# Attention and gated MLP on one core: side tiles for remade columns, earlier loads for the last rows, another split of the last row

## The chip, the core and the metric

The kernel runs on one core of a Trainium2 chip. The time is the device time of one execution in microseconds (us), and the median of the runs counts. Engines: TensorE (PE, with its weight loads PEld), VectorE (DVE), ScalarE (ACT), GpSimd (POOL), and SyncE (SP), which issues most of the transfers. Each engine works through its own list of instructions in a fixed order; an instruction that waits holds up those behind it on its engine.

## What is computed

The input x has 2048 rows of 512. Two branches read its layer norm; the result joins them.

```python
xn = _layernorm(x, axis=-1)
s = _A_ref(xn, A_wqkv, A_wo)      # attention: 32 heads of 16, each row looks at 8 rows
                                  # (itself and 2, 4, ... 14 rows back), softmax, then @ wo
g = _silu(_B_ref(xn, ...))        # below
return x + s * g

# _B_ref: F = 1792, Fh = 896
z = _gelu(x @ w_in)
z1 = z[..., :Fh]
z2 = _layernorm(z[..., Fh:], axis=-1)
g = einsum("ts,bsf->btf", w_sp, z2) + b_sp[None, :, None]   # 2048 x 2048 times 2048 x 896
return (z1 * g) @ w_out
```

Everything is float32.

## The kernel before

**Products.** Each product splits its operands into a high and a low part of type F32R and adds three matmuls (high x high, high x low, low x high). The splitting is done by ACT (the high part, a copy, line 195) and DVE (the low part, a subtraction, line 197) after a raw block has come in (line 169). Raw blocks lie in a ring of four buffers, `raws`; the parts of one block in *side tiles*, `wts`, with a tag for high (`wh`) and one for low (`wl`). Eight *wide* buffers (`t4`) of 128x1024 hold whatever is large: the rows of z2 (`zt_j`), sums, biases, gates (`sg_i`) and x rows (`x3_i`) by turns.

**Stages, in the order PE meets them.** The projection to q, k and v (L385 to L387), whose results leave through `stage` tiles to DRAM. For some columns the layer norm is remade: `xs_k` is high plus low, times a row statistic `rb`, split again (L497 to L502). The rows of z2 (L699 to L727): PE fills PSUM banks in turn, eight of them, ACT empties each with the gelu (L728), DVE takes statistics (L737, L738) and finishes them for two row tiles at once (`mvz`, L740), POOL turns the variance into a factor and an offset (`nmz`, L741 to L743), ACT normalises (L749), and DVE combines row tiles (L762) that SP stores to `t_d` (L768, L769). The large product with w_sp runs as sums of block products (`g`, L820) whose bank starts from a bias seed that ACT writes (L838), with block sums `sa`, `sb`, `sr` made on DVE (L393) and stored to `sums_d`. The product with w_out gives b (L1062 to L1075), stored to `b_d`. At the end comes the product of the attention rows with wo (`s`, the same lines L1062 to L1064 of the projection helper).

**The last stage (L1078 to L1125).** Rows are taken in pairs of 128-row tiles, i = 0, 2, ... 14, in four groups of two pairs. A group's attention rows `ol` are loaded (L802) and split into `o_0h`, `o_0l` to `o_3h`, `o_3l`. For each pair the gate `sg_i` and the x rows come in (`fetch_pair`, L1084 and L1085), the gate goes through silu on ACT (L1107), DVE multiplies the product by the gate (L1117) and adds x (L1122, or L1119 for the last pair), and the result is stored (L1123, L1120). A pair's two loads are *paced*: they wait for a given group's o_3h on ACT. The very last row is done in two pieces, so that the first can be finished while PE makes the second.

**Attention.** It runs on DVE and POOL beside all this, in 32 units of low priority (`attention()`). A unit loads keys and queries (L552, L553), multiplies (`pr`, L573) and sums (`lg`, L580), masks the logits of the first rows by memsets (L595), makes the softmax, weighs the values (`pv`, L617) and adds them up, and stores to `o_d` (L642). Most of its tiles have one buffer.

**Order.** The program is written in source order with priorities, and a scheduler that simulates the engines sets each engine's list. So an edit can move instructions far from its own lines.

Of the kernel before, what the change touches and what calls it, by code (L numbers as in the profile page):

```python
# [57 lines left out]
def kernel(  # L58
# [419 lines left out]
    for j in range(11, NT):  # L478
        if j + 2 < NT:
            fetch_cols(j + 2)  # L480
        if j == NT - 3:
            rb = raws.tile([P, 512], F32, tag="raw", name="rb", bufs=RAW)
            rbv = rb.rearrange("p (j q) -> p j q", j=JC)
            pin(nc.sync.dma_start(rbv, mv_d[:JC, 1].unsqueeze(0).to_broadcast([P, JC, P])))
        turned = column_tile(j)
        if j == 12:
            for i in range(HT - 2):
                pool_sums(1, i, early_tile, turned, SYNC)
        low_x(j - 1, cols[j - 1])
        if j % 2:  # L490
            pair(0, j - 5)
# [38 lines left out]
    def attention():  # L530
# [15 lines left out]

        def load_qk(u):
            sub, h = units[u]
            ks[u] = ap_.tile([P, HWIN, CS], F32, tag="k", name=f"k_{sub}_{h}")
            qs[u] = ap_.tile([P, NH, CS], F32, tag="q", name=f"q_{sub}_{h}")  # L550
# [37 lines left out]
        def shifted(u):  # L588
            sub, h = units[u]
            n = NH * HS  # L590
            lg = lgs[u]
            for w in range(1, W):
                if DIL * w > h * NH:
                    front = min(DIL * w - h * NH, NH) * HS
                    line(nc.vector.memset(lg[0:1, W - 1 - w, :front], MASKED))  # L595
# [179 lines left out]
    for i in range(HT + 2):  # L775
        if i in (1, 3):
            raw_sums(1, HT - 2 + i // 2)
        if i < HT:
            raw_z[i] = [t4(f"zt_{j}").rearrange("p i t -> p (i t)")[:, :FH] for j in (i, HT + i)]
            for h in range(2):  # L780
                for j, zt in zip((i, HT + i), raw_z[i]):
                    z2_half(j, h, zt)
                if i == HT - 1 and h == 0:
                    spatial[0, 1] = spatial_block(0, 1)
        if i == 5:
            b_a = t4("b_a")
# [292 lines left out]
        return t.rearrange("(p j) d -> p j d", j=NT)[:, j : j + 2, :]  # L1079

    def fetch_pair(i, after=None):
        gt, xt = t4(f"sg_{i}"), t4(f"x3_{i}")
        for ins in (
            nc.sync.dma_start(gt, b_d[rows_of[i] // 2]),  # L1084
            nc.sync.dma_start(xt, rows_at(x, rows_of[i])),  # L1085
        ):
            if after:
                tc.add_manual_dep(ins.ins, after.ins.name, SYNC, reason="paced")
        return gt, xt
# [9 lines left out]
    for i in range(0, NT, 2):  # L1099
# [5 lines left out]
        gt, xt = fetched[i]  # L1105
        gt, xt = fetched[i]
        nc.scalar.activation(gt, gt, AF.Silu)  # L1107
        for a in range(2):
            jj = (j0 + a) % NJ
            last = i + a == NT - 1  # L1110
            for p_ in range(1 + last):
                cols_ = slice(p_ * D // 2, (p_ + 1) * D // 2) if last else slice(0, D)
                psu = proj(
                    KB, lambda k: [t[:, jj * P : (jj + 1) * P] for t in os_[k]], wos, f"s_{j0 + a}_{p_}", cols_
                )
                gc, xc = gt[:, a, cols_], xt[:, a, cols_]
                nc.vector.tensor_tensor(gc, psu[:, cols_], gc, op=ALU.mult)  # L1117
                if i == NT - 2:
                    nc.vector.tensor_tensor(gc, gc, xc, op=ALU.add)  # L1119
                    (nc.scalar if p_ else nc.sync).dma_start(outr[j0 + a][:, cols_], gc)  # L1120
        if i < NT - 2:
            nc.vector.tensor_tensor(gt, gt, xt, op=ALU.add)  # L1122
# [45 lines left out]
```

## Time and profile before

| | us |
|---|---|
| median of 3 runs (698.87, 699.14, 701.0) | 699.14 |
| the profiled execution | 696.9 |
| its span | 695.1 |
| PE busy | 686.5 (99%) |
| DVE busy | 624.6 (90%) |
| ACT busy | 278.0 (40%) |
| POOL busy | 213.9 (31%) |

A row of the timeline or of the chain of waits reads: start, duration, engine, line, operation, output and inputs, sizes, number of instructions merged, and in brackets how long the engine had been idle before it and what ended that. A row of the waits reads: who waited for whom, us in total, times, longest. Where PE is busy nearly all the time, its few gaps and the stretch after its last matmul are what other engines can still change.

The z2 stage lies between 217 and 295 us, the large product until about 590, b until 645, the last stage from there to the end.

### The profile page before, as it was taken

How to read it: one execution, taken by the hardware profiler on the slowest of the kernel's cores; microseconds unless marked ns; L12 is line 12 of the kernel's file. 1: busy time of each engine (PE TensorE's matmuls, PEld its weight loads, DVE VectorE, ACT ScalarE, POOL GpSimd, SP SyncE). 2: the span in 40 equal slices, each digit the busy share in tenths (PEclk: the TensorE clock that was granted, in tenths of full speed). 3: DMA queues.
4: the chain of work that ended last, by engine and by line, in shares of the span. 5: the costliest groups of instructions: out<-in, count | busy, mean ns of one | idle time of the engine just before them, and what ended most of it. 6: DMA issues, size and time to landing. Idle time of an engine off the chain costs nothing.

```text
span 695.1 us, 9253 instructions
## 1 busy us (share of the span) xinstructions
PE 686.5 (99%) x3084; PEld 572.8 (82%) x3084; DVE 624.6 (90%) x890; ACT 278.0 (40%) x458; POOL 213.9 (31%) x242
## 2 busy tenths in 40 slices
PE   8999999999999999999999999999999999999996
PEld 7888888888888889987888888888888888888885
DVE  6777867999999979899999999999999999999865
ACT  4342233314424256866524544433344354212431
POOL 3105836372443222123213221223101202552410
PEclk9999999999999999999999999999999999999999
DMA  8769899969999756265899868675585693564897
GB/s 267 255 195 287 293 359 378 339 208 368 400 412 358 321 207 200 81 213 195 288 387 309 288 222 287 206 273 203 160 303 190 211 323 125 182 189 173 266 289 285
DMA packets 102080, 182.37 MB, mean 262 GB/s; under 512 B 9168, under 2 KB 45264, under 8 KB 102032
## 3 DMA queue, kind: packets, MB, share of 16 engines
q1 hardware_dynamic: 56480, 102.14, 43.7%
q0 software_dynamic: 13824, 52.24, 20.9%
q10 hardware_dynamic: 31728, 27.40, 11.7%
q8 instruction: 24, 0.39, 0.2%
q14 instruction: 24, 0.20, 0.1%
HBM read 122.42 MB, written 59.32 MB: 261 GB/s over the span
## 4 chain that ended last, share of the span: by engine, by line
PE 82%; DMA 6%; DVE 4%; ACT 3%; issue 2%; SPq 1%; POOL 1%; DVEq 0%; ACTq 0%
PE g L820 36%; PE qkv L385 6%; PE qkv L386 6%; PE qkv L387 6%; PE z L699 4%; PE z L698 4%; PE z L700 4%; PE b L1063 3%; PE b L1062 3%; PE b L1064 3%; DMA sg<-b_d 3%; PE z L727 2%; PE z L726 2%; PE z L725 2%; DMA ol<-o_d 2%
## 5 line engine op out<-in xcount | busy, mean ns | idle before, releaser
L628 POOL TENSOR_TENSOR pv<-pv 128x1024 f32<-128x1024 f32 x29 | 69.6, 2399 | 100.9 <-DVE pv L617 89.8
L617 DVE TENSOR_TENSOR pv<-v,lg 128x2048 f32<-128x2048 f32 x32 | 74.6, 2332 | 1.2 <-DMA v<-qkv_d 0.6
L573 DVE TENSOR_TENSOR pr<-k,q 128x2048 f32<-128x2048 f32 x32 | 73.6, 2300 | 1.3 <-DMA k<-qkv_d 1.1
L580 DVE TENSOR_REDUCE lg<-pr 128x128 f32<-128x2048 f32 x32 | 73.0, 2280 | 0.1
L642 POOL DMA_DIRECT2D o_d<-tt x32 | 18.0, 562 | 139.3 <-DVE tt L641 139.0
L433 ACT ACTIVATE stage<-qkv 128x512 f32<-128x512 f32 x40 | 23.0, 591 | 29.7 <-DMA qkv_d<-stage 15.3
L1073 ACT ACTIVATE bt<-b 128x512 f32<-128x512 f32 x16 | 9.4, 597 | 47.0 <-PE b L1064 47.0
L802 POOL DMA_DIRECT2D ol<-o_d x32 | 17.7, 555 | 33.3 <-DVE o_2l L197 9.0
L704 ACT ACTIVATE z1t<-z 128x512 f32<-128x512 f32 x28 | 15.5, 596 | 25.7 <-DMA z_d<-z1t 15.1
L727 PE MATMUL z<-w_0h,BIG 128*128 128x512 f32 x64 | 25.1, 391 | 0.0
L726 PE MATMUL z<-w_0l,BIG 128*128 128x512 f32 x64 | 25.0, 391 | 0.0
L280 DVE TENSOR_TENSOR xT<-xT,mr 128x512 f32<-128x512 f32 x20 | 14.9, 743 | 11.3 <-DMA mr<-mv_d 6.3
L725 PE MATMUL z<-w_0h,BIG 128*128 128x512 f32 x64 | 24.9, 389 | 0.0
L737 DVE BATCH_NORM_STATS2 zst<-zt 128x6 f32<-128x448 f32 x32 | 19.3, 614 | 6.1 <-ACT zt L728 6.0
L749 ACT ACTIVATE zt<-zt,nmz,mvz 128x896 f32<-128x896 f32 x16 | 17.5, 1128 | 16.7 <-POOL nmz L743 16.7
L633 DVE TENSOR_TENSOR pv<-pv 128x512 f32<-128x512 f32 x32 | 22.9, 717 | 0.0
L728 ACT ACTIVATE zt<-z 128x512 f32<-128x512 f32 (+1 forms) x32 | 15.9, 535 | 15.0 <-DMA sums_d<-sa 12.0
L727 PE MATMUL z<-w_1h,BIG 128*128 128x384 f32 x64 | 21.5, 336 | 0.0
L725 PE MATMUL z<-w_1h,BIG 128*128 128x384 f32 x64 | 21.5, 336 | 0.0
L726 PE MATMUL z<-w_1l,BIG 128*128 128x384 f32 x64 | 21.4, 335 | 0.0
L393 POOL TENSOR_TENSOR sb<-sa,sb 128x512 f32<-128x512 f32 x12 | 19.5, 1623 | 5.4 <-DMA sb<-in_w_sp 5.0
L741 POOL TENSOR_TENSOR mvz<-mvz,nhalf 128x2 f32<-128x2 f32 x8 | 7.5, 937 | 42.6 <-DVE mvz L740 42.6
(476 smaller groups left out, 2306.6 us busy)
## 6 DMA issues: line engine op xcount, KB each, us to landing
qkv_d<-stage ACTq DMA_DIRECT2D x24, 512.0 KB
v<-qkv_d POOLq DMA_DIRECT2D x14, 704.0 KB, 5.8
k<-qkv_d POOLq DMA_DIRECT2D x13, 704.0 KB, 5.9
sums_d<-sa POOLq DMA_DIRECT2D x14, 512.0 KB, 7.9
sums_d<-sb POOLq DMA_DIRECT2D x14, 512.0 KB, 7.7
z_d<-z1t ACTq DMA_DIRECT2D x14, 512.0 KB
zl<-z_d SPq DMA_DIRECT2D x12, 512.0 KB
tr<-t_d SPq DMA_DIRECT2D x12, 384.0 KB
```

The lines of the kernel that those rows point to most:

```text
L385: nc.tensor.matmul(pq, xh[:, k], wh, start=k == 0, stop=False)
L386: nc.tensor.matmul(pq, xh[:, k], wl, start=False, stop=False)
L387: nc.tensor.matmul(pq, xl[:, k], wh, start=False, stop=k == KB - 1)
L573: line(nc.vector.tensor_tensor(pr, taps(ks[u], j0), qb.unsqueeze(1).to_broadcast([P, W, NJ * CS]), op=ALU.mult))
L580: line(nc.vector.tensor_reduce(lgs[u][:, :, j0 * HS : (j0 + NJ) * HS], pr.rearrange("p w (i d) -> p w i d", d=DH), axis=AX.X, op=ALU.add,))
L617: line(nc.vector.tensor_tensor(pv.rearrange("p w (i d) -> p w i d", d=DH), taps(vs[u], j0).rearrange("p w (i d) -> p w i d", d=DH), lgs[u] ...
L628: eng.tensor_tensor(pv[:, 0:4], pv[:, 0:4], pv[:, 4:8], op=ALU.add)
L698: nc.tensor.matmul(pz, wh[:, cc], xh, start=k == 0, stop=False)
L725: nc.tensor.matmul(pz, xh[:, k], wh, start=k == 0, stop=False)
L726: nc.tensor.matmul(pz, xh[:, k], wl, start=False, stop=False)
L727: nc.tensor.matmul(pz, xl[:, k], wh, start=False, stop=k == KB - 1)
L820: nc.tensor.matmul(pg, z[a], w[b], start=start and i == 0, stop=stop and i == 2, skip_group_check=seeded)
```

## The change

It has seven parts.

1. The row statistic `rb` moves from the raw ring to a small tile of its own, and the remade columns `xs_k` from the raw ring to side tiles.
2. Unit 1 of the attention loads keys and queries into a `pv` tile instead of the single `k` and `q` buffers.
3. The masks of the units that begin at a first row are written by fewer memsets: rows that are masked entirely by one, the others as before.
4. The bias `b_a` is taken from the wide buffers in round 3 of the z2 loop instead of round 5.
5. The x rows of the last pair are fetched into two side tiles ahead of wo's weights; pair 14 has no load of x any more.
6. The loads of pairs 12 and 14 are paced on the third group's rows (`groups[2]`) instead of the fourth's.
7. The last row's pieces are 384 and 128 columns (F3 is 384) instead of 256 and 256.

```diff
@@ remade columns
-            rb = raws.tile([P, 512], F32, tag="raw", name="rb", bufs=RAW)
+            rb = t2("rb", 1, tag="tz", bufs=1)
...
-        xs = raws.tile([P, 512], F32, tag="raw", name=f"xs_{k}", bufs=RAW)
+        xs = wts.tile([P, 512], F32, tag=f"w{'hl'[k % 2]}", name=f"xs_{k}")
@@ attention, load_qk
+            if u == 1:
+                both = ap_.tile([P, W, NJ * CS], F32, tag="pv", name="kq_1")
+                both = both.rearrange("p w (i c) -> p (w i) c", c=CS)
+                ks[u], qs[u] = both[:, :HWIN], both[:, HWIN : HWIN + NH]
+            else:
...
@@ attention, masks
-            for w in range(1, W):
+            full = max(0, W - (h + 1) * NH // DIL)
+            if full:
+                line(nc.vector.memset(lg[0:1, :full], MASKED))
+            for w in range(1, W - full):
                 if DIL * w > h * NH:
-                    front = min(DIL * w - h * NH, NH) * HS
+                    front = (DIL * w - h * NH) * HS
@@ z2 loop
-        if i == 5:
+        if i == 3:
             b_a = t4("b_a")
@@ last stage
+        if i < NT - 2:
+            xt = t4(f"x3_{i}")
+            loads.append(nc.sync.dma_start(xt, rows_at(x, rows_of[i])))
+            whole_x, xt = xt, [xt[:, a] for a in range(2)]
+        else:
+            whole_x, xt = None, last_x
...
+    last_x = [wts.tile([P, D], F32, tag=f"w{n}", name=f"x_last_{n}") for n in "hl"]
+    for a in range(2):
+        nc.sync.dma_start(last_x[a], xr[(NT // JC - 1) * JC + JC - 2 + a])
...
-            fetched[i + 4] = fetch_pair(i + 4, arrived[groups[min(i // NJ + 1, 3)]])
+            fetched[i + 4] = fetch_pair(i + 4, arrived[groups[min(i // NJ + 1, 2)]])
...
-                cols_ = slice(p_ * D // 2, (p_ + 1) * D // 2) if last else slice(0, D)
+                cols_ = (slice(0, F3), slice(F3, D))[p_] if last else slice(0, D)
```

In the new kernel the line numbers of the z2 stage are 9 higher (L740 is L749, L749 is L758) and those of the last stage 8 to 15 higher (L802 is L811, L1084 is L1092, L1123 is L1138).

**SP at the end.** The issues from the last group's attention rows (`ol_3`) on, before and then after.

```order
L802 DMA ol_3<-o_d 32x4x128 x2
L1123 DMA out<-sg 128x1024
L1123 DMA out<-sg 128x1024
L1084 DMA sg<-b_d 128x1024
L1085 DMA x_12<-in_x 128x1024
L1084 DMA sg<-b_d 128x1024
L1085 DMA x_14<-in_x 128x1024
L1123 DMA out<-sg 128x1024
L1123 DMA out<-sg 128x1024
L1120 DMA out<-sg 128x512
```

```order
L811 DMA ol_3<-o_d 32x4x128 x2
L1092 DMA sg<-b_d 128x1024
L1095 DMA x_12<-in_x 128x1024
L1138 DMA out<-sg 128x1024
L1092 DMA sg<-b_d 128x1024
L1138 DMA out<-sg 128x1024
L1138 DMA out<-sg 128x1024
L1138 DMA out<-sg 128x1024
L1135 DMA out<-sg 128x512
L1135 DMA out<-sg 128x384
```

The gates of pairs 12 and 14 (`sg<-b_d`) move ahead of one and of two of the result stores, and the load of x_14 is gone.

**ACT at the end.** The silus (`sg<-sg`) and the high parts of the groups' attention rows, before and then after.

```order
491 L195 ACTIVATE o_0h<-ol_0 128x512
492 L1075 DMA b_d<-bt 128x1024
493 L1107 ACTIVATE sg<-sg 128x1024
494 L195 ACTIVATE o_1h<-ol_1 128x512
495 L1107 ACTIVATE sg<-sg 128x1024
496 L1107 ACTIVATE sg<-sg 128x1024
497 L195 ACTIVATE o_2h<-ol_2 128x512
498 L195 ACTIVATE o_0h<-ol_0 128x512
499 L195 ACTIVATE o_3h<-ol_3 128x512
500 L195 ACTIVATE o_1h<-ol_1 128x512
```

```order
492 L1122 ACTIVATE sg<-sg 128x1024
493 L195 ACTIVATE o_0h<-ol_0 128x512
494 L1122 ACTIVATE sg<-sg 128x1024
495 L1122 ACTIVATE sg<-sg 128x1024
496 L195 ACTIVATE o_1h<-ol_1 128x512
497 L195 ACTIVATE o_2h<-ol_2 128x512
498 L195 ACTIVATE o_3h<-ol_3 128x512
499 L195 ACTIVATE o_0h<-ol_0 128x512
500 L195 ACTIVATE o_1h<-ol_1 128x512
```

The third group's o_1h, o_2h and o_3h now stand together behind the silus of pairs 4 and 6; before, o_1h stood ahead of these and o_3h behind the fourth group's o_0h.

**DVE at the first mvz of the z2 stage.** From the last attention work ahead of it on, before and then after (`sa`, `sb` and `sr` are block sums of w_sp).

```order
260 L393 TENSOR_TENSOR sr_6_1_8r<-sr_6_1_0r,sr_6_1_8r 128x512
261 L737 BN_STATS zst<-zt 128x6
262 L393 TENSOR_TENSOR sb_6<-sa_6,sb_6 128x512
263 L738 BN_AGGR mvz<-zst 128x2
264 L641 STREAM_TRANSPOSE tt_0<-pv_0 128x256
265 L737 BN_STATS zst<-zt 128x6 x2
266 L393 TENSOR_TENSOR sr_6_1_0r<-sr_6_0_0r,sr_6_1_0r 128x512
267 L738 BN_AGGR mvz<-zst 128x2
268 L737 BN_STATS zst<-zt 128x6 x2
269 L738 BN_AGGR mvz<-zst 128x2
270 L393 TENSOR_TENSOR sr_6_0_0r<-sr_6_0_0r,sr_6_1_8r 128x512
271 L740 TENSOR_SCALAR mvz<-mvz 128x2
```

```order
252 L579 TENSOR_TENSOR pr_0<-k_0,q_0 128x2048
253 L642 TENSOR_TENSOR pv_0<-pv_0 128x512
254 L746 BN_STATS zst<-zt 128x6 x2
255 L643 TENSOR_TENSOR pv_0<-pv_0 128x4x2x32
256 L746 BN_STATS zst<-zt 128x6 x2
257 L747 BN_AGGR mvz<-zst 128x2
258 L650 STREAM_TRANSPOSE tt_0<-pv_0 128x256
259 L747 BN_AGGR mvz<-zst 128x2
260 L393 TENSOR_TENSOR sb_6<-sa_6,sb_6 128x512
261 L749 TENSOR_SCALAR mvz<-mvz 128x2
```

The finishing step of the first statistics (`TENSOR_SCALAR mvz`) now comes directly after them and one sum; three `sr` sums and the statistics of the next row tiles stand behind it. On ACT both normalisations that follow from it now stand ahead of the gelu that empties the bank of `z_1_0`, where before they stood behind the gelus of z_1, z_9, z_2_0 and z_10_0.

More of the change, by code (lines that the diff above doesn't have):

```diff
@@ L548, in load_qk @@
             sub, h = units[u]
-            ks[u] = ap_.tile([P, HWIN, CS], F32, tag="k", name=f"k_{sub}_{h}")
-            qs[u] = ap_.tile([P, NH, CS], F32, tag="q", name=f"q_{sub}_{h}")
+            if u == 1:
[3 more added lines that the diff above has]
+            else:
+                ks[u] = ap_.tile([P, HWIN, CS], F32, tag="k", name=f"k_{sub}_{h}")
+                qs[u] = ap_.tile([P, NH, CS], F32, tag="q", name=f"q_{sub}_{h}")
             queue = nc.gpsimd if u > 2 else nc.sync
@@ L1081, in fetch_pair @@
     def fetch_pair(i, after=None):
[L1082 to L1086, printed above, removed]
+        gt = t4(f"sg_{i}")
+        loads = [nc.sync.dma_start(gt, b_d[rows_of[i] // 2])]
+        if i < NT - 2:
[4 more added lines that the diff above has]
+            whole_x, xt = None, last_x
+        for ins in loads:
             if after:
                 tc.add_manual_dep(ins.ins, after.ins.name, SYNC, reason="paced")
-        return gt, xt
+        return gt, xt, whole_x
+    last_x = [wts.tile([P, D], F32, tag=f"w{n}", name=f"x_last_{n}") for n in "hl"]
+    for a in range(2):
+        nc.sync.dma_start(last_x[a], xr[(NT // JC - 1) * JC + JC - 2 + a])
     wos = [ut_at(1, f) for f in range(KB)]
@@ L1103 @@
         if i + 4 < NT:
-            fetched[i + 4] = fetch_pair(i + 4, arrived[groups[min(i // NJ + 1, 3)]])
-        gt, xt = fetched[i]
-        gt, xt = fetched[i]
+            fetched[i + 4] = fetch_pair(i + 4, arrived[groups[min(i // NJ + 1, 2)]])
+        gt, xt, whole_x = fetched[i]
         nc.scalar.activation(gt, gt, AF.Silu)
@@ L1115 @@
                 )
[L1116 removed]
+                gc, xc = gt[:, a, cols_], xt[a][:, cols_]
                 nc.vector.tensor_tensor(gc, psu[:, cols_], gc, op=ALU.mult)
@@ L1121 @@
         if i < NT - 2:
-            nc.vector.tensor_tensor(gt, gt, xt, op=ALU.add)
+            nc.vector.tensor_tensor(gt, gt, whole_x, op=ALU.add)
             nc.sync.dma_start(rows_at(out, j0), gt)
```

## The prediction

> **What bounds the kernel.** The page's engine list and the waits of TensorE come first.
>
> ```profile
> PE 686.5 (99%) x3084; PEld 572.8 (82%) x3084; DVE 624.6 (90%) x890; ACT 278.0 (40%) x458; POOL 213.9 (31%) x242
> PE g L820 <- ACT g L838: 1.1, 1, 1.1
> 316.00:641.00 325.00, 325.00 (x1434) 268.95 (x1435) 317.63 (x440) 127.62 (x215) 84.93 (x88) 1.00 0.70 238
> ```
>
> TensorE (PE) is busy 686.5 of 695.1 us and the change takes no matmul from it, so time can only come from the places where it waits and from the tail behind its last matmul. The second row is the largest wait after the start. In the third (a window: us, PE, PEld, DVE, ACT, POOL, clock, DMA, GB/s) PE has no gap in 325 us; VectorE (DVE) works 317.63 of them, but behind PE. Two gaps and the tail are left.
>
> The first gap, in the chain of waits and the timeline:
>
> ```profile
> 310.09 0.61 DVE wsp_0l L197
> 310.72 3.17 DMA wsp_4r<-in_w_sp
> 313.99 0.61 ACT wsp_4h L195
> 315.19 0.59 ACT g L838
> ...
> 312.59 0.64 ACT L195 ACTIVATE wsp_3h<-wsp_3r 128x512 fp32r<-128x512 f32 x1 [5.03 <-DMA wsp_3r<-in_w_sp]
> 314.32 0.39 PE L820 MATMUL g<-wsp_6h,BIG 128*128 128x512 f32 x1
> 315.82 0.50 PE L820 MATMUL g<-wsp_0h,BIG 128*128 128x512 f32 x1 [1.12 <-ACT g L838]
> 316.16 0.39 PE L820 MATMUL g<-wsp_0l,BIG 128*128 128x512 f32 x1
> ```
>
> ACT writes the bias seeds of the second product (g, L838) only after three weight splits whose raw data came late, because SP could fetch them only when DVE, behind its z2 work, had freed the raw buffers. Matmuls of 512 columns otherwise start 0.227 us apart (below), so PE loses 1.50 - 0.23 = 1.27, then 0.34 - 0.23 = 0.11: 1.4 us.
>
> The second gap, at the last group of attention rows:
>
> ```profile
> 665.69 1.72 POOL L802 DMA_DIRECT2D ol<-o_d  x3 [8.81 <-DVE o_2l L197]
> 669.42 0.63 ACT L195 ACTIVATE o_3h<-ol 128x512 fp32r<-128x512 f32 x1 [3.44 <-DMA ol<-o_d]
> 672.08 1.09 SPq L802 DMA_DIRECT2D ol<-o_d  x2
> 679.39 0.63 ACT L195 ACTIVATE o_3h<-ol 128x512 fp32r<-128x512 f32 x1 [0.98 <-DMA ol<-o_d]
> 679.71 0.39 PE L1064 MATMUL s<-BIG,o_2l 128*128 128x512 f32 x1
> 681.13 0.39 PE L1062 MATMUL s<-BIG,o_0h 128*128 128x512 f32 x1
> ```
>
> Four steps from 679.71 to 681.13 should take 0.91 and took 1.42: 0.5 us. The chain runs backwards: o_3h of the last group waits for its load (issued 672.08), which stood on SP behind four loads paced on o_3h of the group before (669.42), whose load stood on POOL behind a load held 8.81 us by DVE's o_2l.
>
> The tail:
>
> ```profile
> 680.90 0.42 SPq L1084 DMA_DIRECT2D sg<-b_d  x1
> 686.37 0.39 PE L1064 MATMUL s<-BIG,o_3l 128*128 128x512 f32 x1
> 686.60 0.28 PE L1062 MATMUL s<-BIG,o_0h 128*128 128x256 f32 x1
> 686.85 1.23 DVE L1122 TENSOR_TENSOR sg<-sg,x 128x1024 f32<-128x1024 f32 x1
> 687.95 1.06 ACT L1107 ACTIVATE sg<-sg 128x1024 f32<-128x1024 f32 x1 [2.46 <-DMA sg<-b_d]
> 689.04 0.69 DVE L1117 TENSOR_TENSOR sg<-s,sg 128x512 f32<-128x512 f32 x1 [0.97 <-ACT sg L1107]
> 689.35 0.28 PE L1064 MATMUL s<-BIG,o_3l 128*128 128x256 f32 x1
> 690.38 0.42 DVE L1117 TENSOR_TENSOR sg<-s,sg 128x256 f32<-128x256 f32 x1
> 692.13 0.37 ACTq L1120 DMA_DIRECT2D out<-sg  x1
> ```
>
> PE has row 14 ready at 686.37 + 0.39, but DVE begins it at 689.04: the last pair's gates were asked for at 680.90, landed 7 us later, and the silu ran until 689.0. From the last store's issue to the end of the span are 695.1 - 692.1 = 3.0 us.
>
> **The change, part by part.**
>
> *Gates and x rows of the last pairs.* The gates of pairs 12 and 14 and the x rows of pair 12 are paced on the group before, so SP can issue them some seven us sooner, right behind that group's loads (as soon as pair 6 frees its buffers); the silus of pairs 12 and 14 then run behind the o_3h of 679.39 and are done by about 682. The x rows of pair 14 lie in side tiles, fetched hundreds of us before: nothing on the path, and the SP queue isn't held by them, since their buffers' last readers are long done in the window 316 to 641. Row 14 can then start on DVE when its matmuls and pair 12's addition are done: 686.85 + 1.23 = 688.1 in before, about 687.1 when the silu of pair 12 is early too. Row 15 sets the end.
>
> Its two pieces become 384 and 128 columns. Prices of one matmul by width:
>
> ```profile
> 236.21 0.33 PE L726 MATMUL z<-w_1l,BIG 128*128 128x384 f32 x1
> 236.38 0.34 PE L727 MATMUL z<-w_1h,BIG 128*128 128x384 f32 x1
> 16.15 0.60 PE L228 MATMUL xt<-ident,x 128*128 128x128 f32 x4
> 16.50 0.48 PE L308 MATMUL qkv<-wqkv_0h,BIG 128*128 128x512 f32 x1
> 1.34 3.78 PE L290 MATMUL warm<-ident 128*128 128x128 f32 x16 [1.34 <-POOL ident masks.py:199]
> ```
>
> 384 columns step by 0.17 us; 256 by (689.35 - 686.60)/23 = 0.120. For 128 columns of this type no row exists. The transposes take 0.35/4 = 0.0875, the plain F32 warm-up 3.78/16 = 0.236, and the line through 256 and 384 would give 0.07. I take 0.0875, near the line of the same type; ends 0.06 (half of 256) and 0.236. Piece 0: 686.60 + 12 x 0.173 = 688.7, read at 688.9; DVE's multiply and add at 384 columns, between 0.42 and 0.69, some 0.555 each: 690.0. Piece 1: matmuls end at 688.7 + 12 x 0.0875 = 689.7, read at 689.9; two DVE operations of 0.285 from 690.0: 690.6. Store at 690.7, end 693.7 against 695.1: -1.4 us. At 0.06 DVE still sets 690.6, so -1.45 is the low end; at 0.236 the matmuls end at 691.5, the store goes at 692.3 and the end is 695.3: +0.2.
>
> The Trainium skill ("TensorE: Matmul & The Clock Gate", section "Back-to-back issue gap") gives a sustained spacing of about 81 ns at 128 columns and 131 ns at 512. This trace disagrees at 512 (227 ns); by its 81 ns piece 1 would take an estimated 0.97 us, and the tail would come out the same.
>
> *Pacing at the end, 680.* In the new order POOL's last load of the group before no longer stands behind the next group's, and ACT does this group's o_1h, o_2h, o_3h directly after the silu of pair 6 (about 664). That o_3h can come up to 3.5 us before 669.42, and the whole chain to 672.08 and 679.39 with it. I take -0.5. Ends: -0.5, and +1.4 if the last load arrives no sooner, since PE then merely arrives 1.4 us earlier at the same wait.
>
> *First keys in the pv tile, remade columns in side tiles, memsets.*
>
> ```profile
> L595 DVE MEMSET lg<- x80: 65/78/85, 105.1 to 630.0; 1x32 f32 x32, 1x8 f32 x16, 1x16 f32 x16, 1x24 f32 x16
> 111.17 1.32 DVE L197 TENSOR_TENSOR w_0l<-w_0r,w_0h 128x512 fp32r<-128x512 f32 x1 [4.14 <-ACT w_0h L195]
> 236.59 0.98 ACT L728 ACTIVATE zt<-z 128x512 f32<-128x512 f32 x2 [1.45 <-DMA sums_d<-sb]
> 236.56 0.39 PE L725 MATMUL z<-w_0h,BIG 128*128 128x512 f32 x1
> 247.09 0.17 DVE L740 TENSOR_SCALAR mvz<-mvz 128x2 f32<-128x2 f32 x1
> 248.61 2.16 ACT L749 ACTIVATE zt<-zt,nmz,mvz 128x896 f32<-128x896 f32 x2 [5.77 <-POOL nmz L743]
> 246.22 0.39 PE L725 MATMUL z<-w_0h,BIG 128*128 128x512 f32 x1
> ```
>
> Memsets fall from 80 to 56: 24 x 78 ns = 1.9 us of DVE, none of it on PE's path, as the 325-us window shows. The 4.14 us that DVE idles before 111.17 can be filled: unit 1's keys no longer wait for unit 0's buffers, the wqkv raw loads go ahead, and in the new order w_0h stands ahead of the evictions that ACT was held by. I estimate a lead of 3 us for DVE, of at most 4.14 plus a few memsets; at worst 0. None of it is time by itself.
>
> *The z2 stage.* Here the order changes most. DVE now does the first mvz before ten sums and before the next tiles' statistics; ten operations between 236 and 247 stood ahead of it that no longer do. ACT does both first normalisations (L749) before it empties z_1_0's bank, which PE needs again at 246.22. With sb_6, sa_6 x2 and three sr_6 sums (0.6 each) and five statistics behind it, and four operations in their place, mvz comes about 3 us sooner, at 244; with the lead, 241. The normalisations start 1.5 later (as 247.09 to 248.61) and take 2.16, z_1_0's eviction 0.5: 245.2, a us ahead of PE. I take 0; without the lead it is 248.2, +2.0. zt_0 moves to a buffer whose store ends at 236.5 where PE needs z_0_0's bank at 236.56: up to +0.5, 0 with the lead.
>
> b_a is taken two rounds sooner, so zt_12 moves to the buffer of zt_1, and that is free only when its t_d store has landed:
>
> ```profile
> 265.72 0.37 SPq L768 DMA_DIRECT2D t_d<-zt  x1
> 267.90 0.57 ACT L728 ACTIVATE zt<-z 128x512 f32<-128x512 f32 x1
> ```
>
> The store starts 2.2 us before z_12_0's eviction, so it costs some tenths of ACT at most, and nothing with the chain ahead.
>
> *The gap at 314.* It goes when the vector chain is 1.4 us ahead; the changed z2 order and the lead both give more. I take -1.4; ends -1.4 and 0, the chain being just as late. Next late there would be wsp_0l, ready at 310.7, five us ahead. At the start of g the new DVE order has one more z2 operation ahead of wsp_1l; I have no term for it, since the lead covers a half us.
>
> Sum: -1.4 - 0.5 - 1.4 = -3.3 us. The profiled execution took 696.9 (span 695.1 and 1.8 around it), so 693.6; the median of the runs, 699.14, lies 2.2 above it, and I carry that: 695.8.
>
> **Rivals.** A change of 0.3%, about what a measurement of this kernel can tell from none, is 2.1 us.
> - R1, the 314 gap stays: for it, the splits wait for raw buffers and a 3.17 us load, whatever z2 does; against it, DVE's place in that chain. 699.14 - 0.5 - 1.4 = 697.2, the same.
> - R2, 128 columns cost like the F32 warm-up: for it, no such row in this type; against it, the line through 256 and 384. Tail +0.2: 699.14 - 1.4 - 0.5 + 0.2 = 697.4, the same.
> - R3, the normalisations ahead of z_1_0 block ACT: if mvz is not sooner than 247.09, the eviction ends at 248.61 + 2.16 + 0.5 = 251.3, and PE waits 5.1 us, 0.5 more for z_0_0's bank; the 314 gap is absorbed in that. 699.14 - 3.3 + 5.6 = 701.4: slower. It decides for slower from an mvz at about 246.9. For it, the 5.77 us for which ACT waited; against it, the sums that now stand behind mvz.
> - R4, the last o_3h comes no sooner: 699.14 - 1.4 = 697.7, the same. For it, the gates and x rows now share its time on the queues: the load of 680.90 shared its 7 us with three others, so three more transfers in that stretch could hold the last o_3h up by some 3 us, an estimate, which makes 700.7 and is still within 0.3%. The Trainium skill ("DMA: Bandwidth & Descriptors", section "Queues, rings and completion order") says that a DMA engine goes round-robin between its queue rows, which speaks for such a delay of the loads that POOL issued; no run here shows it yet.
>
> **Chances.** Forecast 0.52; R1 0.08; R2 0.14; R3 0.16; R4 0.10. Faster 0.52, same 0.32, slower 0.16. The forecast by itself reaches from 694.4 (all terms at their low ends, and the runs' scatter of 1 us) to 697. The range that holds 8 in 10 reaches from 694.4 into R4 with contention and the mildest of R3, 700.8.
>
> **What would show it.** PE's waits without ACT g at 314; silus of pairs 12 and 14 before 683; DVE's row 14 at 687 to 688; the first mvz near 241 and z_1_0's next bank without a wait; the narrow matmuls 0.09 apart; the last store 1.5 us after the last matmul. A PE wait in z2 on ACT's zt, or narrow matmuls at 0.2, would make the prediction wrong.

## The result, and the profile after

| | before | after |
|---|---|---|
| median, us (12 runs each) | 698.29 | 707.59 |
| lowest and highest run | 696.02, 701.0 | 700.77, 712.09 |
| profiled execution | 696.9 | 706.1 |
| its span | 695.1 | 704.3 |

The changed kernel is slower: ratio 1.012, 95% interval 1.0096 to 1.0144. The prediction of 695.8 us (694.4 to 700.8), faster, was wrong. Runs in a slower state of the chip are left out of the ratios: here the one of 712.09, and below two of some 710 us of the kernel with DVE's order put back.

Page and waits of the changed kernel first. The rows of the waits are: who waited for whom, us in total, times, longest.

```profile
PE 690.4 (98%) x3084; PEld 574.3 (82%) x3084; DVE 623.6 (89%) x866; ACT 277.1 (39%) x458; POOL 224.2 (32%) x242
```

```profile
PE z L707 <- ACT z1t L713: 6.7, 2, 6.2
PE qkv L387 <- DVE BIG L234: 1.0, 1, 1.0
POOL pv L637 <- ACT stage L433: 15.4, 1, 15.4
```

The wait for ACT g, 1.1 us before, is no longer in the list. In its place stands 6.7 us for ACT's z1t, in a stage that the prediction did not look at: the first half of the product with w_in, whose banks ACT empties into `z1t` (L704 before, L713 after). The timeline of PE and ACT there, after:

```profile
208.42 0.39 PE L709 MATMUL z<-BIG,w_5l 128*128 128x512 f32 x1
215.04 0.79 PE L707 MATMUL z<-BIG,w_lasth 128*128 128x512 f32 x1 [6.23 <-ACT z1t L713]
215.63 0.63 PE L708 MATMUL z<-BIG,w_lasth 128*128 128x512 f32 x1
219.90 0.63 PE L709 MATMUL z<-BIG,w_lastl 128*128 128x512 f32 x1
...
214.39 1.08 ACT L713 ACTIVATE z1t<-z 128x512 f32<-128x512 f32 x2 [9.86 <-DMA sums_d<-sb]
```

Before, the matmuls of this place followed each other without a gap. Now PE loses 215.04 - 208.42 - 0.23 = 6.4 us, and what follows is slow too: ten matmuls start (219.90 - 215.63)/10 = 0.427 us apart instead of 0.227, and the first and the last of the slow stretch lie between these two. That is 2.7 us more, so the place costs 9.1. ACT stood for 9.86 us ahead of its z1t: the wide buffer it was to write was, by the record, still being read by a late store of a block sum (`sums_d<-sb`).

Where PE's matmul starts differ most, after against before:

| place | us |
|---|---|
| wait at 208 and the slow matmuls behind it | +9.1 |
| 48.9, for DVE's transposed rows (in no other profile here) | +1.3 |
| 164, for z1t | +0.7 |
| 580 | +1.0 |
| the gap at 314, gone | -1.4 |
| the gap at 680, 0.5 to 0.2 | -0.3 |
| tail, from row 15's first matmul to the end of the span, 8.50 to 7.04 | -1.5 |
| sum (the span grew by 9.2) | +8.9 |

So gains of about the forecast size came in this execution (the one at 314 by another cause than the forecast's, as told below), and one wait that was not forecast is three times as large as all of them.

**Where the wait comes from.** Followed backwards, in the chain of waits (start, us, what) of the changed kernel:

```profile
163.57 0.85 DVE w_0l L197
165.67 0.46 SPq L398
166.85 15.76 DMA sb<-in_w_sp
182.70 0.69 DVE sb L393
204.10 9.76 DMA sums_d<-sb
```

DVE's block sums (DVE adds some sets, POOL others) are asked for by SP at 165 to 167; the load takes 15.8 us, DVE adds at 182.7, and a store that left at 204.1 ends at 213.9. SP issues sums only behind loads into the raw ring, and those wait for DVE's split of w_0. SP and DVE before, then after:

```profile
155.33 0.64 DVE L197 TENSOR_TENSOR w_0l<-w_0r,w_0h 128x512 fp32r<-128x512 f32 x1
155.24 1.09 SPq L169 DMA_DIRECT2D w_1r<-in_w_in  x2
157.46 0.38 SPq L398 DMA_DIRECT2D sa<-in_w_sp  x1
```

```profile
163.49 0.92 DVE L197 TENSOR_TENSOR w_0l<-w_0r,w_0h 128x512 fp32r<-128x512 f32 x1
159.20 5.57 SPq L169 DMA_DIRECT2D w_1r<-in_w_in  x2
165.24 0.38 SPq L398 DMA_DIRECT2D sa<-in_w_sp  x1
```

The split is 8.2 us later and the loads 7.8. Two things that part 2 moved lie ahead of it. On DVE the multiplication `pr` of a further attention step now stands ahead of the splits of w_4, w_5 and w_0. On POOL the first fold of the values (`pv`, L628 before, L637 after) now stands ahead of the fifth set of block sums that POOL adds, and its operand comes late: DVE writes it from 119.52 to 121.81 (the rows put the wait down to ACT's `stage`, which ended at about that time). POOL's timeline and a window, before:

```profile
109.26 1.31 POOL L393 TENSOR_TENSOR sb<-sa,sb 128x512 f32<-128x512 f32 x1
113.72 1.62 POOL L393 TENSOR_TENSOR sb<-sa,sb 128x512 f32<-128x512 f32 x1
127.68 2.40 POOL L628 TENSOR_TENSOR pv<-pv 128x1024 f32<-128x1024 f32 x1 [11.09 <-ACT stage L433]
```

```profile
140.00:157.00 17.00, 17.00 (x77) 14.09 (x76) 16.79 (x23) 2.33 (x5) 12.09 (x10) 1.00 0.62 206
```

and after:

```profile
121.95 2.41 POOL L637 TENSOR_TENSOR pv<-pv 128x1024 f32<-128x1024 f32 x1 [15.37 <-ACT stage L433]
130.80 2.47 POOL L393 TENSOR_TENSOR sb<-sa,sb 128x512 f32<-128x512 f32 x1
```

```profile
140.00:157.00 17.00, 17.00 (x77) 14.08 (x76) 16.71 (x16) 3.99 (x7) 16.87 (x14) 1.00 0.49 169
```

Before, POOL finished the fifth of its six sets (109 to 115) and then idled for the fold; after, it idles 15.4 us for the fold with two sets still to do. The windows (us, PE, PEld, DVE, ACT, POOL, clock, DMA share, GB/s) show that from 140 to 157 POOL is busy 16.9 us instead of 12.1, with sums that DVE must run beside. DVE's 128x2048 multiplication in that window, and behind it when POOL has done:

```profile
151.64 3.37 DVE L579 TENSOR_TENSOR pr<-k,q 128x2048 f32<-128x2048 f32 x1
164.34 2.28 DVE L579 TENSOR_TENSOR pr<-k,q 128x2048 f32<-128x2048 f32 x1
```

I read this as contention between the two engines: in all sixteen profiles this multiplication takes 2.27 to 2.30 us where no operation of POOL overlaps it, and each one of 2.4 us or more stands beside one. The Trainium skill ("GPSIMD Engine Reference", section "Key points") says that GpSimd shares its interfaces to SBUF with VectorE and contends with its instructions of two SBUF inputs, with which these rows agree. So DVE is slowed, its split is later still, and later DVE runs dry, since the sums that it should add have not come. Windows as above, before and after:

```profile
170.00:183.00 13.00, 13.00 (x59) 10.78 (x58) 12.90 (x21) 2.65 (x6) 5.09 (x6) 1.00 1.03 413
```

```profile
170.00:183.00 13.00, 13.00 (x59) 10.78 (x58) 5.47 (x6) 2.55 (x5) 2.40 (x1) 1.00 1.05 409
```

DVE does 5.5 us of work in 13 instead of 12.9. I read the wait at 208 as these 7.5 us come back; this last link is read from the chain of waits and was not tested by itself.

All this is a reading of one pair of traces. The experiments test the two orders. The expectations call A the theory that the keys' place (part 2) makes the loss, by POOL's order (A1), by the place itself (A2) or by DVE's splits that hold SP (A3). B is the theory that the side tiles of part 1 make it. Every kernel below computes all that the reference does.

### The profile page after: what moved, and what is told of

It reads as the page before. It is cut to its first block, busy times and chain, and to the rows that moved or that the text cites. A ratio compares the mean times of both kernels' runs of the same rounds, so it can differ in the third digit from the quotient of the medians.

```text
span 704.3 us, 9224 instructions
## 1 busy us (share of the span) xinstructions
PE 690.4 (98%) x3084; PEld 574.3 (82%) x3084; DVE 623.6 (89%) x866; ACT 277.1 (39%) x458; POOL 224.2 (32%) x242
## 4 chain that ended last, share of the span: by engine, by line
DVE 39%; DMA 22%; PE 18%; issue 13%; ACT 3%; POOL 3%; SPq 1%; DVEq 0%; ACTq 0%; POOLq 0%
DVE lg L586 5%; DVE pr L579 4%; DVE pv L626 4%; DMA qkv_d<-stage 4%; PE b L1072 3%; PE b L1071 3%; PE b L1073 3%; DVE BIG L197 3%; DMA sb<-in_w_sp 2%; DMA wsp_9r<-in_w_sp 2%; PE s L1073 2%; PE s L1072 2%; PE s L1071 2%; DVE pv L642 2%; DMA x<-in_x 2%
## 5 line engine op out<-in xcount | busy, mean ns | idle before, releaser
L637 POOL TENSOR_TENSOR pv<-pv 128x1024 f32<-128x1024 f32 x29 | 69.6, 2400 | 102.0 <-DVE pv L626 86.6
L579 DVE TENSOR_TENSOR pr<-k,q 128x2048 f32<-128x2048 f32 x30 | 72.0, 2400 | 5.8 <-DMA k<-qkv_d 5.6
L713 ACT ACTIVATE z1t<-z 128x512 f32<-128x512 f32 x28 | 15.4, 595 | 42.9 <-DMA z_d<-z1t 19.3
L811 POOL DMA_DIRECT2D ol<-o_d x32 | 17.7, 555 | 25.5 <-DVE o_0l L197 5.4
L758 ACT ACTIVATE zt<-zt,nmz,mvz 128x896 f32<-128x896 f32 x16 | 17.5, 1131 | 15.3 <-POOL nmz L752 15.3
L197 DVE TENSOR_TENSOR BIG<-zt,BIG 128x512 fp32r<-128x512 f32 (+2 forms) x24 | 18.6, 782 | 4.4 <-ACT BIG L195 4.3
L393 POOL TENSOR_TENSOR sb<-sa,sb 128x512 f32<-128x512 f32 x12 | 21.3, 1777 | 3.2 <-DMA sb<-in_w_sp 2.8
```

Of the source, the lines that this page charges most:

```text
L197: lows.append(pin(nc.vector.tensor_tensor(lo, src, hi.bitcast(F32), op=ALU.subtract)))
L579: line(nc.vector.tensor_tensor(pr, taps(ks[u], j0), qb.unsqueeze(1).to_broadcast([P, W, NJ * CS]), op=ALU.mult))
L637: eng.tensor_tensor(pv[:, 0:4], pv[:, 0:4], pv[:, 4:8], op=ALU.add)
```

## Experiments: which part makes the loss

**Without the keys.** The changed kernel without part 2.

```diff
-            if u == 1:
-                both = ap_.tile([P, W, NJ * CS], F32, tag="pv", name="kq_1")
-                both = both.rearrange("p w (i c) -> p (w i) c", c=CS)
-                ks[u], qs[u] = both[:, :HWIN], both[:, HWIN : HWIN + NH]
-            else:
-                ks[u] = ap_.tile([P, HWIN, CS], F32, tag="k", name=f"k_{sub}_{h}")
-                qs[u] = ap_.tile([P, NH, CS], F32, tag="q", name=f"q_{sub}_{h}")
+            ks[u] = ap_.tile([P, HWIN, CS], F32, tag="k", name=f"k_{sub}_{h}")
+            qs[u] = ap_.tile([P, NH, CS], F32, tag="q", name=f"q_{sub}_{h}")
```

> The changed kernel with only part 2 (unit 1's keys and queries in the pv tile) undone. Theory A: this part alone moves the attention one unit forward in VectorE's list, so the weight splits w_0 stand one unit later, SP is held by the raw ring 5.6 us ahead of the first block sums' loads, VectorE then waits 8 us for them, and TensorE waits 6.2 us for ACT's z1t near 208 and runs 2.5 us at half clock behind it. Then this kernel has no TensorE wait above 1 us between 200 and 225, and comes to 694 to 697 us, 2 to 4 below the kernel before. Theory B: the side tiles of part 1 let loads and stores collide between 80 and 120 us and part 2 is innocent. Then the wait near 208 stays and the time is 704 to 709.

Measured: 700.39 us, 1.0029 (1.0005 to 1.0052). The wait near 208 is gone, and POOL's sixth set ends earlier than before (143 against 149). The gain is not the whole of what the other parts promised, though: PE waits at 314 (1.9), 394 (1.4), 559 (1.3) and 684 (1.3 in all).

**The keys alone.** The kernel before with part 2 (the diff above, turned round).

> The kernel before with part 2 alone. Theory A: the wait near 208 with its slow stretch is there, 706 to 710 us. Theory B: no such wait, 698 to 700 us.

Measured: 712.3, 1.0208 (1.0169 to 1.0246). Waits of PE:

```profile
PE z L704 <- ACT z1t L710: 5.6, 2, 3.9
```

Part 2 by itself makes a loss larger than the whole change does, in the same stage and by the same kind of wait (4.1 us at 163 and 1.9 at 212, with slow matmuls behind the first). These make about 8 of the 15 us by which its span is longer; the rest is spread over waits at 568, 582 and 692 and a tail of 9.6. The wait at 163 comes from POOL: by the record ACT's first z1t had waited 12.2 us for the store of POOL's last sums, which left at 159.5 (156.7 in the changed kernel, 153.4 in the kernel before). Together the two runs settle that part 2 makes most of the loss: 9.3 us by the medians with it, 2.8 without.

**The other parts alone, or without their partners.** The old end in the changed kernel (parts 5 to 7 undone):

```diff
-    last_x = [wts.tile([P, D], F32, tag=f"w{n}", name=f"x_last_{n}") for n in "hl"]
...
-            fetched[i + 4] = fetch_pair(i + 4, arrived[groups[min(i // NJ + 1, 2)]])
+            fetched[i + 4] = fetch_pair(i + 4, arrived[groups[min(i // NJ + 1, 3)]])
...
-                cols_ = (slice(0, F3), slice(F3, D))[p_] if last else slice(0, D)
+                cols_ = slice(p_ * D // 2, (p_ + 1) * D // 2) if last else slice(0, D)
```

> The changed kernel with parts 5, 6 and 7 (the end) undone. If the end is worth what its steps show (the stretch from row 15's first matmul to the end was 8.5 us before and is 7.0 in the changed kernel), it is 1.5 to 2 us slower than the changed kernel, some 709 us; if the earlier loads were of no use, it equals the changed kernel.

Measured: 705.58, 1.0112 (1.0065 to 1.0158), with the large wait for z1t (5.0 us) in it. The loss does not need the new end, and undoing the new end costs nothing that can be measured here (the medians' interval is wide). In the profiled execution of this kernel the last gate came early enough: its silu ended 1.0 us after row 15's first matmul (2.4 in the kernel before), and the tail was 7.06 us, as short as with the new end.

The new end alone on the kernel before (the same diff turned round):

> The kernel before with parts 5, 6 and 7 alone. Nothing of it stands ahead of 317 us, so Theory A and B alike expect no wait near 208 and a tail shorter by 1.5: 696.5 to 697 us. Over 698 would say that the loads asked for earlier take back at the last o_3h what the tail gains.

Measured: 698.55, 1.0003 (0.9978 to 1.0029). The tail is 7.02, 1.5 shorter, as forecast, but the wait for the last o_3h is longer, 1.5 us in all instead of 0.5. PE and ACT there:

```profile
680.75 0.50 PE L1062 MATMUL s<-BIG,o_3h 128*128 128x512 f32 x1 [0.98 <-ACT o_3h L195]
680.07 0.63 ACT L195 ACTIVATE o_3h<-ol 128x512 fp32r<-128x512 f32 x1 [1.19 <-DMA ol<-o_d]
```

That is the prediction's R4: o_3h came no sooner, and PE waited longer for it.

The side tiles alone (part 1 on the kernel before):

```diff
-            rb = raws.tile([P, 512], F32, tag="raw", name="rb", bufs=RAW)
+            rb = t2("rb", 1, tag="tz", bufs=1)
...
-        xs = raws.tile([P, 512], F32, tag="raw", name=f"xs_{k}", bufs=RAW)
+        xs = wts.tile([P, 512], F32, tag=f"w{'hl'[k % 2]}", name=f"xs_{k}")
```

> The kernel before with part 1 alone (rb and the remade columns out of the raw ring). With everything but the keys the time was 1.0029 of before and with the end alone 1.0003; so if part 1 carries that cost, 1.001 to 1.004 here, and its profile has a gap at 314 of 1.8 us or more and weight waits between 390 and 560 like the run without keys; else 0.998 to 1.001.

Measured: 700.2, 1.0032 (1.0007 to 1.0057). The expected gap at 314 did not come; instead PE waited 2.3 us at 681.5 for the last o_3h, with slow matmuls behind it (1.7), and 0.7 at two other places. So part 1 has a small loss of its own, clear of the interval.

The masks alone (part 3 on the kernel before):

```diff
-            for w in range(1, W):
+            full = max(0, W - (h + 1) * NH // DIL)
+            if full:
+                line(nc.vector.memset(lg[0:1, :full], MASKED))
+            for w in range(1, W - full):
...
```

> The kernel before with part 3 alone: 24 memsets of 78 ns fewer, 1.9 us of VectorE. The prediction held them at nothing on the path: 0.998 to 1.001 of before. If VectorE's time passes to the end, 0.997.

Measured: 696.08, 0.9986 (0.9965 to 1.0006): nothing that can be told from no change.

The changed kernel without parts 1 and 2 (their two diffs, undone):

> The changed kernel with parts 1 and 2 undone (masks, bias, end remain). Alone, the masks gave 0.9986 and the end 1.0003 of the kernel before. If the losses of the change lie in parts 1 and 2 only, 695 to 697 us, a ratio of 0.996 to 0.999, and no TensorE wait between 160 and 230; if parts 3 to 7 hold a loss of their own, over 1.001.

Measured: 698.42, 1.0005 (0.9986 to 1.0023). The gain expected at the end did not show in the total: the tail is 6.99, but PE waits at 296 (0.9), 323 (0.7), 558 (1.7) and 575 (0.6). Part 4 was not run by itself; it is among the parts that make 1.0005 here.

## Experiments: how the keys make it

**POOL's order put back.** The changed kernel, and one edge for the scheduler (no wait on the chip, since both stand on POOL): the first fold behind the last addition of POOL's fifth set.

```diff
-            eng.tensor_tensor(out_, p_, q_, op=ALU.add)
+            ins = eng.tensor_tensor(out_, p_, q_, op=ALU.add)
+        if eng is nc.gpsimd:
+            pool_adds.append(ins)
...
-            eng.tensor_tensor(pv[:, 0:4], pv[:, 0:4], pv[:, 4:8], op=ALU.add)
+            ins = eng.tensor_tensor(pv[:, 0:4], pv[:, 0:4], pv[:, 4:8], op=ALU.add)
+            if part[:2] == (0, 0):
+                tc.add_manual_dep(ins.ins, pool_adds[4].ins.name, NOSYNC, reason="sums ahead")
```

> The changed kernel, keys still in the pv tile, with one ordering edge more: GpSimd's first fold of the attention (L637) may stand in its list only behind the fifth set of block sums, as it did before the change; VectorE's list falls back too, the splits w_0 ahead of the seventh pr. Theory A1 (GpSimd's list: in the changed kernel it idles 15 us, 106.6 to 122, in front of that fold with block sums behind it, finishes them among VectorE's work, and the z1 tiles and wide buffers come free 5 us late): no TensorE wait above 1.5 us near 208, 697 to 701 us. Theory A2 (the keys' place itself, their loads at 91 and 103 us and the attention one unit ahead): wait stays, 704 to 709.

Measured: 697.13, 0.9991 (0.9967 to 1.0015). The timelines of POOL, SP and DVE and the window of 170 to 183 of this kernel:

```profile
124.93 2.41 POOL L641 TENSOR_TENSOR pv<-pv 128x1024 f32<-128x1024 f32 x1
154.38 0.38 SPq L402 DMA_DIRECT2D sa<-in_w_sp  x1
151.66 0.92 DVE L197 TENSOR_TENSOR w_0l<-w_0r,w_0h 128x512 fp32r<-128x512 f32 x1
153.82 2.28 DVE L583 TENSOR_TENSOR pr<-k,q 128x2048 f32<-128x2048 f32 x1
```

```profile
170.00:183.00 13.00, 13.00 (x59) 10.76 (x58) 10.35 (x15) 2.58 (x5) 4.56 (x6) 1.00 1.04 415
```

The fold starts 3 us later, POOL does not idle ahead of it, SP loads the sums at 154.4 instead of 165.2, DVE has 10.4 us of work in the 13 us window instead of 5.5, and no wait near 208 is left. One line of order gives back 707.59 - 697.13 = 10.5 us by the medians (9 by the ratios) with the keys still in the `pv` tile, which rules A2 out as the main cause. It does not part POOL from DVE, though: the scheduler moved DVE's list back as well, and the split of w_0 stands ahead of that `pr` again, as the last two rows of the timeline show.

**DVE's order put back instead.** The changed kernel with an edge on DVE: the seventh `pr` of the attention behind the second of the two splits of w_0 that stood ahead of it before. POOL's order stays that of the changed kernel.

```diff
-            line(nc.vector.tensor_tensor(
+            scored.append(line(nc.vector.tensor_tensor(
...
+    tc.add_manual_dep(scored[6].ins, lows[base_ + 1].ins.name, NOSYNC, reason="splits ahead")
```

> The changed kernel with one ordering edge more, on VectorE alone: the seventh pr stands behind the split of w_0's second block, as before the change; GpSimd's first fold stays ahead of the fifth set. Theory A1: GpSimd is as late as in the changed kernel, so 703 to 708 us and a wait of 3 us or more near 208. Theory A3 (VectorE's list is the cause: splits behind one more unit hold SP's queue by the raw ring): the block sums' loads go out 5 to 7 us sooner, the wait near 208 is below 1.5 us, and 697 to 701.

Measured: 700.47, 1.0045 (1.002 to 1.0069). POOL and SP of this kernel:

```profile
116.94 2.40 POOL L639 TENSOR_TENSOR pv<-pv 128x1024 f32<-128x1024 f32 x1 [12.78 <-issue]
157.18 0.38 SPq L398 DMA_DIRECT2D sa<-in_w_sp  x1
```

POOL still idles 12.8 us for the fold, but the sums are loaded at 157.2, as before the change, and the wait near 208 is gone. 7 us come back by the medians, 5 by the ratios. So POOL's order alone is not enough to make the loss: A1 as I had put it falls with this run, and A3 is half right.

**POOL's order alone, in the kernel before.** The edge turned round: POOL's fifth set behind the first fold.

```diff
...
+            if part[:2] == (0, 0):
+                tc.add_manual_dep(pool_adds[4].ins, ins.ins.name, NOSYNC, reason="sums behind")
```

> The kernel before with one ordering edge: GpSimd's fifth set of block sums stands behind the first fold of the attention. No keys are moved, VectorE's list keeps its splits. Theory A1: GpSimd idles until 127, the sums end late, TensorE waits for z1t, 703 to 712 us. Theories A2 and A3: 697 to 699, as before.

Measured: 701.23, 1.0045 (1.003 to 1.0059). Timeline of POOL and waits of PE:

```profile
125.81 2.40 POOL L632 TENSOR_TENSOR pv<-pv 128x1024 f32<-128x1024 f32 x1 [10.80 <-DVE pv L621]
```

```profile
PE z L731 <- ACT z1t L710: 1.0, 1, 1.0
PE z L731 <- ACT zt L734: 1.0, 1, 1.0
```

POOL's order by itself costs 3 us, by small waits after 217, where A3 had it at nothing. DVE's order makes the rest where POOL's stands as in the changed kernel: DVE's put back alone brought 1.012 down to 1.0045, the ratio of POOL's order alone, and with both back it is 0.999. DVE's order moved alone was not run, so whether it costs anything without POOL's stays open.

All sixteen profiles fit this but one. Seven `pr` stand ahead of the split of w_4 in the changed kernel, with the keys alone and with the old end, whose ratios are 1.011 to 1.021; six in all the others, none above 1.0052. Ahead of its first fold POOL makes 16 additions in those three and in the two kernels at 1.0045, 17 without the keys and with the side tiles alone (1.0029 and 1.0032), and 20 in the rest, at 0.9986 to 1.0008 (the exception, at 1.0052, is the last kernel of this section). So the side tiles move POOL's fold too, ahead of three additions; that this is their 0.3% is not shown.

A table of what each kernel's trace shows in that stretch (us, starts):

| kernel | POOL's last addition of its sixth set | first load of sums on SP | first z1t on ACT | DVE idle for sums, 120 to 235 | ratio |
|---|---|---|---|---|---|
| before | 147.5 | 157.5 | 158.8 | 0 | 1 |
| after | 152.9 | 165.2 | 164.2 | 7.5 | 1.012 |
| keys alone | 157 | 165.4 | 166.8 | 5.9 | 1.021 |
| POOL's order alone | 150 | 159.9 | 161.2 | 2.0 | 1.0045 |
| DVE's order put back | 149 | 157.2 | 158.5 | 2.8 | 1.0045 |
| POOL's order put back (DVE's with it) | 142 | 154.4 | 155.7 | 4.7 | 0.999 |
| no keys | 140 | 154.0 | 153.2 | 2.7 | 1.003 |

Where SP loads the sums at 165, the ratio is 1.012 and more; at 154 to 160 it is 0.999 to 1.0045. DVE's idle time alone does not order the kernels.

**POOL's order put back, without the side tiles.** Part 1 undone in the kernel that gave 697.13.

> The changed kernel with part 1 undone, the keys in the pv tile, and the ordering edge on GpSimd's fold. If the keys are harmless once the lists are put back, it equals the run without keys and without side tiles within 0.2%, 695 to 697 us; if the early loads of unit 1 cost something of themselves, 0.3% or more above it.

Measured: 700.76, 1.0052 (1.0024 to 1.008), where I had expected no difference. Its profiled execution (697.7, below the median) shows waits of 0.9 at 217, for z1t, and 1.0 at 557. So with the old raw ring the keys keep a cost that the edge does not remove. What it is stays open.

## Experiments: the end, and the gap at 314

The new end with the old pacing, on the kernel before (parts 5 and 7; the diff is against the new end alone):

```diff
-            fetched[i + 4] = fetch_pair(i + 4, arrived[groups[min(i // NJ + 1, 2)]])
+            fetched[i + 4] = fetch_pair(i + 4, arrived[groups[min(i // NJ + 1, 3)]])
```

> The kernel before with the last x rows in side tiles and the 384/128 split, but pairs 12 and 14 paced on the last group as before. The change's pacing gains if the gates' landing sets the tail, loses if it holds up the last o_3h (TensorE's wait at 680 was 0.5 us before, 1.6 in the end-alone run). Forecast: the wait at 680 back to 0.5, the last silu at about 687.5, the tail 0.7 to 1 us shorter than before: 0.5 to 1 us below the kernel before, equal to or below the end-alone run.

Measured: 699.64, 1.0008 (0.9985 to 1.0031), tail 9.35 where some 7.5 to 7.8 was expected: the last silu ends 3.5 us after row 15's first matmul.

Then the kernel with POOL's order put back once more, and beside it the same kernel with the old pacing (the diff just above).

> The changed kernel with the one edge on GpSimd's list again, over more rounds, as the candidate that may beat both. Its one profile had a TensorE wait of 1.0 us left (314) and none at 680. If the terms of the prediction hold once GpSimd's and VectorE's lists are put back (-1.4 tail, -0.5 at 680, -0.4 to -1.4 at 314), 695 to 696.5 against 698 for the kernel before, a ratio near 0.997. If the keys in the pv tile cost something of their own, 698 or more.

> The same kernel with pairs 12 and 14 paced on the last group, as before the change. If the pacing gives the tail its 1.4 us, this one is 0.7 to 1.5 us above the one with pacing, its last silu after 686 and its row 14 on VectorE waiting for it; if pacing is worth nothing, equal.

Measured: 697.34, 0.9994 (0.9973 to 1.0016), tail 6.97; and with the old pacing 697.88, 0.9997 (0.9974 to 1.0019), tail 7.73. The first DVE operation of row 14, with the new pacing and with the old:

```profile
687.90 0.69 DVE L1138 TENSOR_TENSOR sg<-s,sg 128x512 f32<-128x512 f32 x1 [0.84 <-PE s L1079]
```

```profile
690.50 0.69 DVE L1138 TENSOR_TENSOR sg<-s,sg 128x512 f32<-128x512 f32 x1 [0.64 <-ACT sg L1128]
```

With the new pacing DVE waits for PE, with the old for ACT's silu. In the eight profiles with the new pacing, the last silu ends 0 to 1.6 us ahead of row 15's first matmul and the tail is 6.97 to 7.06; in the eight with the old, it ends 1.0 to 3.5 after it and the tail is 7.06 to 9.6. So the pacing takes the silu out of the tail. Yet no total shows it: other gaps vary by as much between executions. The clearest is the gap at 314. Two executions of one and the same kernel, the one with POOL's order put back, had it at 1.0 us (in the first of the two comparisons) and at 2.1 (in the second). The matmuls there, in the second, and in the kernel with the old pacing:

```profile
314.08 0.39 PE L835 MATMUL g<-wsp_6h,BIG 128*128 128x512 f32 x1
316.28 0.50 PE L835 MATMUL g<-wsp_0h,BIG 128*128 128x512 f32 x1 [1.81 <-ACT g L853]
316.62 0.39 PE L835 MATMUL g<-wsp_0l,BIG 128*128 128x512 f32 x1
```

```profile
314.42 0.39 PE L835 MATMUL g<-wsp_6h,BIG 128*128 128x512 f32 x1
316.87 0.79 PE L835 MATMUL g<-wsp_0h,BIG 128*128 128x512 f32 x1 [2.07 <-ACT g L853]
317.89 0.63 PE L835 MATMUL g<-wsp_0h,BIG 128*128 128x512 f32 x1
```

No version that was run beats the kernel before by more than its interval; the lowest median is that of the masks alone.

## Why the prediction was wrong, step by step

- *First keys, "at worst 0": the step that failed.* "I estimate a lead of 3 us for DVE ... at worst 0. None of it is time by itself" costed part 2 by a wait of DVE that it would fill, and put its cost at nothing. In its place the runs show a loss: the change cost 9.3 us with part 2 and 2.8 without, by the medians, through POOL's fold and DVE's `pr` that now stand ahead of what they hold up, and through ACT and PE behind these. The lists that part 2 reorders between 100 and 165 us (POOL's fold and sums, DVE's splits) were not read against each other, and of the places shown only the ends and z2 were. No rival had this place. The forecast also took "PE has no gap" in a stage for slack: the stage up to 217 had no gap before because SP's loads came 8 us sooner, and no row that I read said how near the next wait was.
- *The gap at 314, -1.4: gone by luck in this execution, and R1 was right.* It was to go because the vector chain would be ahead. In the changed kernel the first mvz came at 248.09, 1.0 us later than before (241 was forecast), and ACT's seed started at 324.08, 8.9 us later; the gap closed because PE, held up at 208, came 11.6 us later still. In the second execution of the kernel with POOL's order put back, mvz came 13 us sooner than before, and the seed no sooner:

```profile
234.06 0.16 DVE L755 TENSOR_SCALAR mvz<-mvz 128x2 f32<-128x2 f32 x1
315.64 2.14 ACT L853 ACTIVATE g<-b_bh 128x512 f32<-128x512 f32 x4
```

  ACT waited 6.1 us there for the raw load of wsp_3 (5.0 before), as R1 had it: whatever z2 does. As a term of a median the gap was wrong as well: it is 0 to 2.2 us over these kernels, and 1.0 and 2.1 in two executions of one. A gap of one execution was counted as if every execution had it.
- *The gap at 680, -0.5, and R4.* 0.2 was left of it in the changed kernel, so -0.3; with the new end alone it grew to 1.5. R4 was right about that kernel, and POOL's order put back gave 0 in one execution and 0.55 in the next.
- *The tail, -1.4.* It measured -1.5. The timeline of the last row, after:

```profile
697.26 0.33 PE L1071 MATMUL s<-BIG,o_0h 128*128 128x384 f32 x1
699.42 0.27 PE L1072 MATMUL s<-BIG,o_0h 128*128 128x128 f32 x1
700.54 0.28 PE L1073 MATMUL s<-BIG,o_3l 128*128 128x128 f32 x1
701.54 0.37 ACTq L1135 DMA_DIRECT2D out<-sg  x1
```

  The narrow matmuls start (700.54 - 699.42)/10 = 0.112 apart, between the ends 0.06 and 0.236; I had taken 0.0875, so R2 fell. That the runs with the old pacing have tails of 7.73 and 9.35 with the new pieces, and 7.06 with the old ones when the silu happened to be early, shows that the sooner silu carries this term and hardly the narrow piece. With the silu ending 1.9 us after row 15's first matmul in both, the tail is 7.73 with the new pieces and 7.99 with the old ones (the side tiles alone), so the narrow piece gives some 0.25.
- *The silus of pairs 12 and 14.* The prediction had them done by 682, that is 4.6 us ahead of row 15's first matmul in before's times. The last one ended at 696.79, 0.5 ahead of it: sooner than before by 2.9, which was enough for DVE to wait for PE alone, but later than worked out.
- *z2 and R3.* PE had no wait in z2; the normalisations ahead of z_1_0 did not block it. R3 was hardly put to the test: its condition, an mvz no sooner than 247.09, came true in the changed kernel (248.09), but PE was 11.6 us late there; with POOL's order put back mvz came at 234, and PE had no wait in z2 either.
- *The sum.* -3.2 of the -3.3 came in this execution, 1.4 of it by luck, and 12 us of new losses were not in it. The low end of the range, 694.4, does not follow from its own terms: their low ends add up to -3.35, which with 1 us of scatter makes 694.8.

## What to carry to other kernels

Where a scheduler sets each engine's list, an edit of one buffer is costed by reading all lists from that place on, and above all what now stands ahead of an operation that waits: here one fold ahead of two sets of sums on POOL, beside one multiplication ahead of splits on DVE, went with a loss of 8 to 9 us, and one line that put the fold back, and by the scheduler the multiplication with it, gave that back. A stage in which TensorE shows no gap may still have no slack: say for each late load of the stage how far ahead of its need it lands before calling a change there free. A gap of some tenths to 2 us that one profiled execution shows is no term of a median until a second execution shows it too.

## What the runs showed of the hardware

- **In these profiles a wait of TensorE costs more than its length from about 2.2 us on.** Waits of 6.39, 5.21, 4.07, 2.31, 2.22 and 2.16 us (from start to start, less the usual 0.227) were each followed by 6 to 12 matmuls at 0.427 us instead of 0.227, 1.2 to 2.7 us in all; behind waits of 2.08, 1.97, 1.87, 1.86 and 1.84 there were none (the two fences of PE at 314 show 1.97 without, 2.22 with). In the changed kernel the profile's clock shows it:

```profile
209.00:222.00 13.00, 6.96 (x19) 5.55 (x20) 12.93 (x20) 5.68 (x8) 4.53 (x5) 0.74 1.02 389
```

  The Trainium skill ("TensorE: Matmul & The Clock Gate", section "Wait — 56ns, not 53.3ns?") puts the throttled start-to-start of 512 columns at 426.7 ns, which agrees with 0.427 here. The same page of the Trainium skill (section "What's actually happening") lets the gate close after an idle window of some 3.4 us that runs freely; the runs differ from that, since matmuls ran slow behind a wait of 2.16.
